# The m tiles' sums ahead of the tail in front, the last m tiles' work in block 0 laid out anew, and k's squares moved

## The chip, the cores and the metric

One core of a Trainium2 chip runs the whole program in one launch. The metric is the device time of that core in microseconds, the median of several executions. The kernel's times, its profile and its trace come from the same chip type. Line numbers (L288) are those of the kernel before.

## The reference

The reference computes a transformer-like block and all its gradients, for 2048 rows of width 512, 32 heads of 16 columns and an MLP of width 1792. In short:

```
xn = layernorm(x)
s  = attention(xn, wqkv) @ wo            # 32 heads, softmax over all 2048 keys
y  = layernorm(xn)
m  = gelu(y @ w1 + b1) @ w2 + b2
out = x + s * silu(m)
outputs: out, and the gradients of x, wqkv, wo, w1, b1, w2, b2 for a given grad_out
```

With `sg = sigmoid(m)` the gate is `m * sg`. The gradient that goes into attention's output is `dso = grad_out * m * sg`, and `dO = dso @ wo^T` is what attention's backward pass needs. The gradient towards m needs `s` and the factor `grad_out * sg * (1 + m * (1 - sg))`, so both `m * sg` and this factor are stored ("GB") for the last phase.

## The kernel before

The rows are cut into 16 tiles of 128, four tiles to a group. The program has three phases: `phase_pre` (layernorms, q, k, v, the MLP forward, the gate, dO), `attention_core` (attention forward and backward together) and `phase3` (the remaining products). Within `phase_pre` and within `attention_core` the order of the instructions on PE, ACT and DVE (in `phase_pre` on POOL too) is the order in which the code issues them; each engine works through its own list in that order and waits where an operand isn't there yet. The DMAs on SP's queue are placed by the framework.

**k's norms.** `kv_tile` makes k, v and q of one tile: three products on PE, three copies out of PSUM on ACT (L170), and after the fourth tile of a group three copies of k and v on POOL (L185 to L187) and a DMA. `k_norm(g, i)` squares k of one tile on POOL (L174) and sums the squares for each head on DVE (L175), through two buffers. The squares of groups 2 and 3 stand behind all of the `kv_tile` steps; behind them come a maximum over all tiles on DVE (L238) and one over the partitions on POOL (L239). The result is used in `row_shift`, which sets a bound for the exponent, much later.

**The MLP's hidden tiles.** `h_tile(g, fc)` is one of 14 tiles of the hidden layer for one group: four matmuls into one of seven PSUM banks (pool `psA`), the bias on DVE (9 of 14) or on ACT (5 of 14) into `h1p`, and for each pair of tiles one gelu on ACT and two DMAs to scratch memory (`H1T_s`, `HGT_s`). `h1p` has four buffers, each for a pair. Between the hidden tiles stand the norms of q (`q_norm`, POOL and DVE as for k) and, in groups 2 and 3, the dO products of tiles 0 to 7 (`do_proj`).

**The m tiles.** `m_tile(t)` issues, for one tile: 14 matmuls into a bank of `psA` (L284), the sum with b2 on DVE (`m_add`, L288), tanh and a scaled copy on ACT for the sigmoid (`m_sig`, L291 and L292), and then the tail on DVE: `m * sg` and `dso` (`m_dso`, L296 and L297) and three operations for the stored factor (`m_grad`, L307 to L309), followed by a DMA on POOL's queue (L310). After the last tile of a group `m_dso` also issues the DMA that transposes dso for the dO products (L301) and one that stores it (L303). Tiles 0 to 3 come after the hidden groups 0 and 1, tiles 4 to 7 after group 2, tiles 8 to 11 after group 3 and `row_shift`.

**Block 0.** Attention runs over 16 pairs of heads and four chunks of 512 queries: 64 blocks of 16 steps, one step for 128 keys. A step has the scores `s` (two matmuls into one of two PSUM slots of two banks, tag "st"), the products `d` (two banks of their own, `d0` and `d1`), the exp of s on ACT (`S`, L892), two products on DVE (`m0`, `m1`, L903) that read d and the exp, and the accumulating matmuls `a1` and `a2`. A second pass over each block, one block behind, uses `t` in the same "st" slots and an exp `T`; in 3 of its 16 steps the exp of t is not computed but the exp of s is transposed (`E`, L848, copied by DVE, `eE`, L853). One more PSUM bank, "z", serves E and the second pass. In block 0 there is no second pass yet, and `first_block` lays out a simpler order: step g issues s of g+2, E of g-1 where g is 4, 8 or 12, d of g+1, a1 of g, place V, a2 of g-1, place W. In the places V (index 0) and W (index 1) `left_over` puts the work on m tiles 12 to 15 and on dO of tiles 8 to 15, all through the z bank: the 14 matmuls of a tile in two halves (`first`, `second`), the sigmoid (`sig`) and the whole tail (`rest`) at V, dO one tile at a time (`do`), and the transpose of dso in four parts (`turn`) on PE, each copied by ACT (L392). dO's copy out of PSUM is on ACT too (L339).

Of the kernel before, what the change touches and what calls it, by code (L numbers as in the profile page):

```python
# [8 lines left out]
bf16 = mybir.dt.bfloat16  # L9
f32 = mybir.dt.float32  # L10
# [7 lines left out]
IC = D // 128  # L18
# [23 lines left out]
def phase_pre(ctx, tc, k, A_x, A_wqkv, A_wo, B_w1, B_b1, B_w2, B_b2, grad_out, opnds, psz, tailp):  # L42
# [157 lines left out]
    with tc.manual_schedule(engines={ET_.PE, ET_.Activation, ET_.DVE, ET_.Pool}):  # L200
        for g in range(2):
            load_x(g)
        nc.scalar.dma_start(out=wqkv_sb[:, :, D:3 * D], in_=wq3[:, :, D:3 * D])
        nc.scalar.dma_start(out=wqkv_sb[:, :, 0:D], in_=wq3[:, :, 0:D])
        nc.scalar.dma_start(out=w1_sb[:], in_=B_w1.rearrange("(c p) f -> p c f", p=128))
        for g in range(4):
            NS[g] = p1.tile([128, NPAIR, 4, 2, NATW], bf16, name="NS", bufs=4)
            nc.gpsimd.memset(NS[g][:, :, :, :, 0:1], 1.0)
        open1(0)
        open1(1)  # L210
        one_a(0, 0)
# [24 lines left out]
        for f, *a in steps:  # L236
            f(*a)
        nc.vector.reduce_max(out=kmaxrun[:], in_=kn2[:].rearrange("p t h -> p h t"), axis=AX.X)  # L238
# [63 lines left out]
        if i == 3:  # L302
            nc.sync.dma_start(out=k.DSO_s[g], in_=dso4[g])  # L303

    def m_grad(t, q, sg, gB):
        g, i = divmod(t, 4)
        nc.vector.scalar_tensor_tensor(out=q, in0=sg, scalar=1.0, in1=gB[:, 0, :], op0=ALU.subtract, op1=ALU.mult)  # L307
        nc.vector.tensor_tensor(out=q, in0=sg, in1=q, op=ALU.subtract)
        nc.vector.tensor_tensor(out=gB[:, 1, :], in0=q, in1=do4[g][:, i, :], op=ALU.mult)  # L309
        nc.gpsimd.dma_start(out=k.GB_s[g, :, i], in_=gB)  # L310

    def load_do(g):
        nc.sync.dma_start(out=do4[g], in_=rows4(go2, g))

    def m_tile(t):
        g, i = divmod(t, 4)
        if i == 0:
            do4[g] = p2.tile([128, 4, D], bf16, name="do4", bufs=1)[:]
            load_do(g)
            dso4[g] = p2.tile([128, 4, D], bf16, name="dso4", bufs=1)[:]  # L320
        m_mm(t, psA.tile([128, 512], f32, name="ps_m", tag="mm"), 0, FC)
        m = p2.tile([128, D], bf16, name="m")[:]
        m_add(t, m)
        th = p2.tile([128, D], f32, name="th")[:]
        sg = p2.tile([128, D], bf16, name="sg")[:]
        m_sig(m, th, sg)
        gB = p2.tile([128, 2, D], bf16, name="gB", bufs=3)[:]
        m_dso(t, m, sg, gB)
        m_grad(t, p2.tile([128, D], bf16, name="q1")[:], sg, gB)

    def do_proj(t, ps_pool=psA, tag="mm"):
# [4 lines left out]
        pd = ps_pool.tile([128, 512], f32, name="pd", tag=tag)  # L336
        for bc in range(IC):
            nc.tensor.matmul(pd[:], lhsT=dsoT[g][:, i, bc, :], rhs=woT[:, bc, :], start=(bc == 0), stop=(bc == IC - 1))
        nc.scalar.copy(out=nd[:, :, i, :], in_=pd[:].rearrange("p (a c) -> p a c", a=NPAIR))  # L339
        if i == 3:  # L340
            ts = slice(4 * g, 4 * g + 4)
            nd0 = nd[:, 0].rearrange("p t (j c) -> p t j c", j=2)
            nc.gpsimd.tensor_copy(out=QPad[:, ts, 2:4, 0:16], in_=nd0)
            if g >= 2:
                turn_q(g)
            nc.sync.dma_start(out=k.NATQd_s[g], in_=nd)
            nc.gpsimd.tensor_copy(out=OP0["NATQd"][:, ts], in_=nd0)

    def left_over(big, mid2, xt2):
# [12 lines left out]
        load_do(3)  # L362
        v = {}

        def z(nm):
            return psz.tile([128, 512], f32, name=nm, tag="z")

        def first(t):
            m_mm(t, z("ps_m15"), 0, 7)

        def second(t):
            m_mm(t, None, 7, FC)
            mq = mid2.tile([128, 2, 512], bf16, name="e")
            v[t] = dict(m=mq[:, 0, :], q=mq[:, 1, :])
            m_add(t, v[t]["m"])

        def sig(t):
            s = mid2.tile([128, 2, 512], bf16, name="e")
            v[t]["sg"] = s[:, 0, :]
            th = xt2.tile([128, 4, 128], f32, name="xt")  # L380
            m_sig(v[t]["m"], th[:].rearrange("p a b -> p (a b)"), v[t]["sg"])

        def rest(t):
            gB = gBs[:, t % 2]
            m_dso(t, v[t]["m"], v[t]["sg"], gB)
            m_grad(t, v[t]["q"], v[t]["sg"], gB)

        def turn(i):
            pt = psz.tile([128, IC, 128], bf16, name="dso_tp", tag="z")
            for b in range(IC):  # L390
                nc.tensor.transpose(pt[:, b, :], dso4[3][:, i, b * 128:(b + 1) * 128], k.ident_bf[:])
            nc.scalar.copy(out=dsoT[3][:, i], in_=pt[:])  # L392

        def do(t):
            do_proj(t, psz, "z")
        return {0: [[], [(first, 12)]], 1: [[], [(second, 12)]], 2: [[(sig, 12)], [(first, 13)]],
                3: [[(rest, 12)], [(second, 13)]], 4: [[(sig, 13)], [(first, 14)]], 5: [[(rest, 13)], [(second, 14)]],
                6: [[(sig, 14)], [(first, 15)]], 7: [[(rest, 14)], [(second, 15)]], 8: [[(sig, 15), (do, 8)], [(do, 9)]],
                9: [[(rest, 15), (do, 10)], [(do, 11)]], 10: [[(turn, 0)], [(turn, 1)]], 11: [[(do, 12)], [(turn, 2)]],
                12: [[(do, 13)], [(turn, 3)]], 13: [[(do, 14)], [(do, 15)]]}  # L400
# [22 lines left out]
    with tc.manual_schedule(engines={ET_.PE, ET_.Activation, ET_.DVE, ET_.Pool}):  # L423
# [5 lines left out]
        for fc in range(FC):  # L429
            h_tile(1, fc)  # L430
            if fc in (2, 4, 7, 9, 12):
                q_norm(qn.pop(0))
        for t in range(4):
            m_tile(t)
        for g in (2, 3):
            for fc in range(FC):
                h_tile(g, fc)
# [2 lines left out]
                elif fc in (1, 3, 5, 6, 8) or fc == 9 and g == 3:  # L440
                    q_norm(qn.pop(0))
            if g == 2:
                for t in range(4, 8):
                    m_tile(t)
# [3 lines left out]
        for t in range(8, 12):  # L448
            m_tile(t)
    c1.close()  # L450
    return left_over

# [322 lines left out]
def attention_core(ctx, tc, opnds, ps_z, tail, NAT_s, NATQ_s, Oall, dQall, dKVT_out, ident_f32, ident_bf, npairs=16, nqc=4, turned=(0, 1, 2)):  # L775
# [286 lines left out]
    p0, v0 = first_block()  # L1062
    pe = joined(p0, unrolled(PE_ORDER))
    dve = joined(v0, unrolled(DVE_ORDER))
    left = tail(gbp, ep, finp)
    act = []
    for g in range(NSTEP + 16):
        if g < NSTEP:
# [187 lines left out]
```

## Time and profile before

| | |
|---|---|
| median of 3 runs | 2359.58 us (2359.49 to 2362.84) |
| the profiled execution | 2358.28 us, of which its span is 2356.5 us |
| PE busy | 2232.8 us (95%) |
| DVE busy | 2025.0 us (86%) |
| ACT busy | 2044.4 us (87%) |
| POOL busy | 315.5 us (13%) |
| mean granted PE clock | 0.986 |

The span is what the trace covers; the 1.8 us beside it lie around it. PE's busy time counts matmuls that overlap in the array once. "Idle before" is the time that an engine stood before an instruction, and the arrow names what ended it. In the rows of the timeline the columns are start, duration, engine, line, operation, output and input tiles, shapes, number of instructions and, in brackets, the idle time.

### The profile page before, as it was taken

How to read it: one execution, taken by the hardware profiler on the slowest of the kernel's cores; microseconds unless marked ns; L12 is line 12 of the kernel's file. 1: busy time of each engine (PE TensorE's matmuls, PEld its weight loads, DVE VectorE, ACT ScalarE, POOL GpSimd, SP SyncE). 2: the span in 40 equal slices, each digit the busy share in tenths (PEclk: the TensorE clock that was granted, in tenths of full speed). 3: DMA queues.
4: the chain of work that ended last, by engine and by line, in shares of the span. 5: the costliest groups of instructions: out<-in, count | busy, mean ns of one | idle time of the engine just before them, and what ended most of it. 6: DMA issues, size and time to landing. Idle time of an engine off the chain costs nothing.

```text
span 2356.5 us, 50896 instructions
## 1 busy us (share of the span) xinstructions
PE 2232.8 (95%) x20082; PEld 796.0 (34%) x20128; DVE 2025.0 (86%) x3600; ACT 2044.4 (87%) x2336; POOL 315.5 (13%) x757
## 2 busy tenths in 40 slices
PE   7887999999999999999999999999999998889698
PEld 3332233333333333333333333333333333334343
DVE  6566899999999999999999999999999996775064
ACT  6564999999999999999999999999999998883143
POOL 4320111111111111111111111111111112100000
PEclk9998999999999999999999999999999999999899
DMA  9775999999999999999999989899999998796961
GB/s 294 226 265 130 173 164 181 171 168 182 164 180 166 184 163 178 168 176 169 177 176 166 183 161 190 158 182 167 178 167 177 156 155 220 192 214 123 187 161 63
DMA packets 1315362, 415.56 MB, mean 176 GB/s; under 512 B 1272241, under 2 KB 1291698, under 8 KB 1313970
## 3 DMA queue, kind: packets, MB, share of 16 engines
q1 hardware_dynamic: 1311362, 401.56, 89.9%
q0 software_dynamic: 2176, 7.34, 0.9%
q8 instruction: 157, 2.57, 0.4%
q10 hardware_dynamic: 1584, 3.41, 0.4%
q14 instruction: 83, 0.68, 0.1%
HBM read 46.52 MB, written 49.03 MB: 41 GB/s over the span
## 4 chain that ended last, share of the span: by engine, by line
PE 74%; DVE 9%; ACT 2%; issue 2%; SPq 2%; DMA 2%; DVEq 0%; ACTq 0%
PE d L886 12%; PE X L923 11%; PE s L864 11%; PE Z L1004 9%; PE X L936 7%; PE Z L996 5%; DVE gts L903 5%; PE t L876 5%; PE ET L848 4%; PE ps_dw L631 2%; PE XT L948 2%; PE X L926 1%; PE ps_dy L686 1%; PE ps_dwkv L736 1%; PE ps_dhg L646 1%
## 5 line engine op out<-in xcount | busy, mean ns | idle before, releaser
L903 DVE TENSOR_TENSOR gts<-d,et 128x512 bf16<-128x512 f32 x2048 | 1321.9, 684 | 79.8 <-PE d L886 25.9
L892 ACT ACTIVATE et<-s 128x1024 bf16<-128x1024 f32 x1024 | 1043.3, 1044 | 17.6 <-PE d L886 13.6
L897 ACT ACTIVATE e<-t 128x1024 bf16<-128x1024 f32 x832 | 866.4, 1042 | 22.0 <-PE t L876 3.5
L886 PE MATMUL d<-QDT,KVT 32*128 32x512 bf16 x2048 | 757.1, 384 | 20.6 <-DVE gts L903 19.5
L864 PE MATMUL s<-QDT,KVT 32*128 32x512 bf16 x2048 | 398.4, 385 | 11.3 <-DVE m L288 8.2
L1004 PE MATMUL Z<-gk,W 128*32 128x512 bf16 x2048 | 397.1, 384 | 0.0
L923 PE MATMUL X<-et,Lc 128*32 128x512 bf16 x2048 | 369.8, 389 | 0.0
L926 PE MATMUL X<-et,NAT 128*32 128x512 bf16 x2048 | 368.7, 388 | 0.0
L936 PE MATMUL X<-gts,NAT 128*17 128x512 bf16 x2048 | 330.9, 382 | 0.0
L996 PE MATMUL Z<-e,W 128*32 128x512 bf16 x1664 | 321.6, 383 | 3.6 <-DVE ob L1023 1.2
L876 PE MATMUL t<-KVT,QDT 32*128 32x512 bf16 x1664 | 323.1, 383 | 1.0 <-ACT e L897 1.0
L886 PEld LDWEIGHTS <-KVT 32*128 32x128 bf16 x2048 | 173.0, 90 | 236.5 <-issue 236.1
L864 PEld LDWEIGHTS <-KVT 32*128 32x128 bf16 x2048 | 106.0, 91 | 255.2 <-issue 230.8
L970 POOL TENSOR_TENSOR W<-NATQd,rL 128x128 bf16<-128x128 bf16 x64 | 25.8, 403 | 1122.0 <-DVE rL L969 1122.0
L1004 PEld LDWEIGHTS <-W 128*32 128x32 bf16 x2048 | 100.3, 94 | 171.8 <-issue 141.3
L876 PEld LDWEIGHTS <-QDT 32*128 32x128 bf16 x1664 | 92.1, 91 | 145.4 <-issue 140.6
L996 PEld LDWEIGHTS <-W 128*32 128x32 bf16 x2048 | 105.2, 94 | 106.8 <-issue 96.5
L923 PEld LDWEIGHTS <-Lc 128*32 128x32 bf16 x2048 | 83.6, 93 | 164.5 <-issue 164.3
L853 DVE COPY eE<-ET 128x1024 bf16<-128x1024 bf16 x192 | 130.2, 678 | 6.1 <-PE ET L848 6.1
L848 PE MATMUL ET<-ident_bf,et 128*128 128x128 bf16 x1536 | 119.0, 220 | 1.3 <-DVE e L288 0.9
L848 PEld LDWEIGHTS <-et 128*128 128x128 bf16 x1536 | 86.7, 98 | 44.7 <-issue 44.7
L936 PEld LDWEIGHTS <-NAT 128*17 128x17 bf16 x2048 | 79.6, 89 | 62.2 <-issue 45.6
(197 smaller groups left out, 2335.4 us busy)
## 6 DMA issues: line engine op xcount, KB each, us to landing
gk<-gts SPq DMA_TRANSPOSE x512, 4.5
H1T_s<-h1p SPq DMA_DIRECT2D x28, 256.0 KB, 3.1
h<-H1T_s SPq DMA_DIRECT2D x28, 256.0 KB, 3.3
HGT_s<-hgT SPq DMA_DIRECT2D x21, 256.0 KB, 2.5
NAT_s<-NS SPq DMA_DIRECT2D x4, 1056.0 KB, 5.7
dKVT_s<-ob SPq DMA_DIRECT2D x16, 256.0 KB, 3.7
gb<-GB_s SPq DMA_DIRECT2D x4, 1024.0 KB, 6.1
Rkv<-dKVT_s SPq DMA_DIRECT2D x2, 2048.0 KB, 13.2
```

The costliest lines, as they stand in the source:

```text
L848: nc.tensor.transpose(ET[:, hj, m * 128:(m + 1) * 128], st_et[g - 3 + m][:, hj, 384:512], ident_bf[:])
L864: nc.tensor.matmul(s[:, hj, :], lhsT=op["KVT"][r, kb * 128:(kb + 1) * 128], rhs=op["QDT"][r, qc * 512:(qc + 1) * 512], start=True, stop=Tr ...
L876: nc.tensor.matmul(t[:, hj, :], lhsT=op["QDT"][r, q0:q0 + 128], rhs=op["KVT"][r, kc * 512:(kc + 1) * 512], start=True, stop=True, tile_pos ...
L886: nc.tensor.matmul(d[:], lhsT=op["KVT"][r, kb * 128:(kb + 1) * 128], rhs=op["QDT"][r, qc * 512:(qc + 1) * 512], start=True, stop=True, til ...
L892: nc.scalar.activation(out=et[:], in_=st_s.pop(g)[:], func=ACT.Exp)
L897: nc.scalar.activation(out=e[:], in_=st_t.pop(g)[:], func=ACT.Exp)
L903: nc.vector.tensor_tensor(out=gts[:, g % 2, hj], in0=st_d.pop((g, hj))[:], in1=st_et[g][:, hj], op=ALU.mult)
L923: nc.tensor.matmul(X[64 + 32 * hj:96 + 32 * hj, :], lhsT=Lc[:, :], rhs=et[:, hj, :], start=(kb == 0), stop=False, skip_group_check=True, t ...
L926: nc.tensor.matmul(X[32 * hj:32 * hj + 32, :], lhsT=NATt[:, kb, hj, 1:33], rhs=et[:, hj, :], start=(kb == 0), stop=(kb == 15), tile_positi ...
L936: nc.tensor.matmul(X[64 + 32 * hj:64 + 32 * hj + 17, :], lhsT=NATt[:, kb, hj, 0:17], rhs=gts[:, kb % 2, hj, :], start=False, stop=(kb == 1 ...
L996: nc.tensor.matmul(Z[32 * hj:32 * hj + 32, :], lhsT=blk[j]["W1"][:, qb, hj, :], rhs=e[:, hj, :], start=(qb == 0), stop=False, tile_positio ...
L1004: nc.tensor.matmul(cur["Z"][32 * hj:32 * hj + 32, :], lhsT=blk[j]["W2"][:, qb, hj, :], rhs=grhs, start=False, stop=(qb == 3), tile_positio ...
```

## The change

- `k_norm` of groups 2 and 3 moves in between the last `kv_tile` steps; the maximum over all tiles moves behind the first hidden tile of group 1.
- `m_tile` becomes `m_group`: within a group of four tiles, a tile's sum and sigmoid are issued ahead of the tail of the tile in front.
- In block 0 the sigmoid is issued right after the sum (with `second`, at W of odd steps), and the tail is split: `rest1` (three DVE operations) at V of the next even step, `rest2` (two, and the DMA) at V of the odd step after it.
- dO is made two tiles at a time, and dso is transposed in one piece, both in the "st" slots of s; each is copied by one ACT instruction. They stand at W of steps 8 to 12.

The core of the diff:

```diff
-        steps += [(n2_c, 3, 0), (n2_c, 3, 1), (kv_tile, 3, 1), (n2_c, 3, 2), (n2_c, 3, 3), (kv_tile, 3, 2), (kv_tile, 3, 3)]
-        steps += [(k_norm, g, i) for g in (2, 3) for i in range(4)]
+        steps += [(n2_c, 3, 0), (n2_c, 3, 1), (kv_tile, 3, 1), (k_norm, 2, 0), (k_norm, 2, 1), (n2_c, 3, 2), (n2_c, 3, 3),
+                  (kv_tile, 3, 2), (k_norm, 2, 2), (k_norm, 2, 3), (k_norm, 3, 0), (k_norm, 3, 1), (kv_tile, 3, 3), (k_norm, 3, 2), (k_norm, 3, 3)]
         for f, *a in steps:
             f(*a)
-        nc.vector.reduce_max(out=kmaxrun[:], in_=kn2[:].rearrange("p t h -> p h t"), axis=AX.X)
-        nc.gpsimd.partition_all_reduce(kmax2[:], kmaxrun[:], channels=128, reduce_op=bass_isa.ReduceOp.max)
...
+    def m_grad1(t, q, sg, gB):
+        nc.vector.scalar_tensor_tensor(out=q, in0=sg, scalar=1.0, in1=gB[:, 0, :], op0=ALU.subtract, op1=ALU.mult)
+
+    def m_grad2(t, q, sg, gB):
         g, i = divmod(t, 4)
         nc.vector.tensor_tensor(out=q, in0=sg, in1=q, op=ALU.subtract)
         nc.vector.tensor_tensor(out=gB[:, 1, :], in0=q, in1=do4[g][:, i, :], op=ALU.mult)
         nc.gpsimd.dma_start(out=k.GB_s[g, :, i], in_=gB)
...
+    def m_group(g):
...
+        prev = None
+        for t in range(4 * g, 4 * g + 4):
+            m_mm(t, psA.tile([128, 512], f32, name="ps_m", tag="mm"), 0, FC)
+            m, sg, q = [p2.tile([128, D], bf16, name=nm)[:] for nm in ("m", "sg", "q1")]
+            gB = p2.tile([128, 2, D], bf16, name="gB", bufs=3)[:]
+            m_add(t, m)
+            m_sig(m, p2.tile([128, D], f32, name="th")[:], sg)
+            if prev:
+                m_dso(t - 1, prev[0], prev[1], prev[3])
+                m_grad(t - 1, prev[2], prev[1], prev[3])
+            prev = m, sg, q, gB
+        m_dso(t, prev[0], prev[1], prev[3])
+        m_grad(t, prev[2], prev[1], prev[3])
...
         def second(t):
             m_mm(t, None, 7, FC)
             mq = mid2.tile([128, 2, 512], bf16, name="e")
...
+            v[t] = mq[:, 1, :], s[:, 0, :], gBs[:, t % 2], mq[:, 0, :]
+            m_add(t, mq[:, 0, :])
             th = xt2.tile([128, 4, 128], f32, name="xt")
+            m_sig(mq[:, 0, :], th[:].rearrange("p a b -> p (a b)"), s[:, 0, :])
+
+        def rest1(t):
+            q, sg, gB, m = v[t]
+            m_dso(t, m, sg, gB)
+            m_grad1(t, q, sg, gB)
+
+        def rest2(t):
+            m_grad2(t, *v[t][0:3])
+
+        def turn(_):
+            pt = st2.tile([128, 4, IC, 128], bf16, name="dso_tp", tag="st")
+            for i in range(4):
+                for b in range(IC):
+                    nc.tensor.transpose(pt[:, i, b, :], dso4[3][:, i, b * 128:(b + 1) * 128], k.ident_bf[:])
+            nc.scalar.copy(out=dsoT[3], in_=pt[:])
 
         def do(t):
...
+            pd = st2.tile([128, 2, 512], f32, name="pd", tag="st")
+            for n in range(2):
+                for bc in range(IC):
+                    nc.tensor.matmul(pd[:, n, :], lhsT=dsoT[g][:, i + n, bc, :], rhs=woT[:, bc, :], start=(bc == 0), stop=(bc == IC - 1))
+            nc.scalar.copy(out=ND[g][:, :, i:i + 2, :].rearrange("p a n c -> p n a c"), in_=pd[:].rearrange("p n (a c) -> p n a c", a=NPAIR))
+            if i == 2:
+                do_done(g)
+        steps = {g: [[], []] for g in range(14)}
+        for n, t in enumerate(range(12, 16)):
+            steps[2 * n][1].append((first, t))
+            steps[2 * n + 1][1].append((second, t))
+            steps[2 * n + 2][0].append((rest1, t))
+            steps[2 * n + 3][0].append((rest2, t))
+        for g, f in ((8, (do, 8)), (9, (do, 10)), (10, (turn, 0)), (11, (do, 12)), (12, (do, 14))):
+            steps[g][1].append(f)
+        return steps
...
             h_tile(1, fc)
             if fc in (2, 4, 7, 9, 12):
                 q_norm(qn.pop(0))
-        for t in range(4):
-            m_tile(t)
+            if fc == 0:
+                nc.vector.reduce_max(out=kmaxrun[:], in_=kn2[:].rearrange("p t h -> p h t"), axis=AX.X)
+                nc.gpsimd.partition_all_reduce(kmax2[:], kmaxrun[:], channels=128, reduce_op=bass_isa.ReduceOp.max)
+        m_group(0)
```

`do_done(g)` holds what `do_proj` did after a group's last tile (the copies on POOL, for groups 2 and 3 the transposing DMA of `turn_q`, and the DMA that stores dO), unchanged.

More of the change, by code (lines that the diff above doesn't have):

```diff
@@ L303, in m_dso @@
             nc.sync.dma_start(out=k.DSO_s[g], in_=dso4[g])
-    def m_grad(t, q, sg, gB):
+    def m_grad1(t, q, sg, gB):
+        nc.vector.scalar_tensor_tensor(out=q, in0=sg, scalar=1.0, in1=gB[:, 0, :], op0=ALU.subtract, op1=ALU.mult)
+    def m_grad2(t, q, sg, gB):
         g, i = divmod(t, 4)
-        nc.vector.scalar_tensor_tensor(out=q, in0=sg, scalar=1.0, in1=gB[:, 0, :], op0=ALU.subtract, op1=ALU.mult)
         nc.vector.tensor_tensor(out=q, in0=sg, in1=q, op=ALU.subtract)
@@ L310, in m_grad, with do_proj @@
         nc.gpsimd.dma_start(out=k.GB_s[g, :, i], in_=gB)
+    def m_grad(*a):
+        m_grad1(*a)
+        m_grad2(*a)
     def load_do(g):
         nc.sync.dma_start(out=do4[g], in_=rows4(go2, g))
[L315 to L331, printed above, removed]
+    def m_group(g):
+        do4[g] = p2.tile([128, 4, D], bf16, name="do4", bufs=1)[:]
+        load_do(g)
+        dso4[g] = p2.tile([128, 4, D], bf16, name="dso4", bufs=1)[:]
+        prev = None
[11 more added lines that the diff above has]
+        m_grad(t, prev[2], prev[1], prev[3])
+    def do_proj(t):
         g, i = divmod(t, 4)
@@ L335, in do_proj @@
         nd = ND[g]
-        pd = ps_pool.tile([128, 512], f32, name="pd", tag=tag)
+        pd = psA.tile([128, 512], f32, name="pd", tag="mm")
         for bc in range(IC):
@@ L340, in do_proj, with do_done, left_over @@
         if i == 3:
[L341 to L349, printed above, removed]
+            do_done(g)
+    def do_done(g):
+        ts = slice(4 * g, 4 * g + 4)
+        nd0 = ND[g][:, 0].rearrange("p t (j c) -> p t j c", j=2)
+        nc.gpsimd.tensor_copy(out=QPad[:, ts, 2:4, 0:16], in_=nd0)
+        if g >= 2:
+            turn_q(g)
+        nc.sync.dma_start(out=k.NATQd_s[g], in_=ND[g])
+        nc.gpsimd.tensor_copy(out=OP0["NATQd"][:, ts], in_=nd0)
+    def left_over(big, mid2, xt2, st2):
         w = [big.tile([128, 2, 16, 128], bf16, name="gk")[:].rearrange("p a b c -> p (a b c)") for _ in range(3)]
@@ L383, in rest @@
[L383 to L392, printed above, removed]
-        def do(t):
[L395 to L400, printed above, removed]
+            m_sig(mq[:, 0, :], th[:].rearrange("p a b -> p (a b)"), s[:, 0, :])
@@ new lines, in do @@
+        def do(t):
+            g, i = divmod(t, 4)
+            pd = st2.tile([128, 2, 512], f32, name="pd", tag="st")
[4 more added lines that the diff above has]
+            if i == 2:
+                do_done(g)
@@ L442, in phase_pre @@
             if g == 2:
-                for t in range(4, 8):
-                    m_tile(t)
+                m_group(1)
         row_shift()
@@ L447, in phase_pre @@
         nc.scalar.activation(out=e_one[:], in_=k.eps_t[:], func=ACT.Exp)
-        for t in range(8, 12):
-            m_tile(t)
+        m_group(2)
     c1.close()
@@ L1064, in attention_core @@
     dve = joined(v0, unrolled(DVE_ORDER))
-    left = tail(gbp, ep, finp)
+    left = tail(gbp, ep, finp, ps_st)
     act = []
```

5 lines of the change are left out of this document (removed).

## The prediction

> **What bounds the kernel now.** I read the page first, then the busy times by stretches, then the timeline of the stretches that the diff touches.
>
> ```profile
> span 2356.5 us, 50896 instructions
> PEclk9998999999999999999999999999999999999899
> ...
> PE 74%; DVE 9%; ACT 2%; issue 2%; SPq 2%; DMA 2%; DVEq 0%; ACTq 0%
> ...
> L892 ACT ACTIVATE et<-s 128x1024 bf16<-128x1024 f32 x1024 | 1043.3, 1044 | 17.6 <-PE d L886 13.6
> ...
> H1T_s<-h1p SPq DMA_DIRECT2D x28, 256.0 KB, 3.1
> ...
> 75.00:80.00 5.00, 4.48 (x11) 1.62 (x11) 3.85 (x6) 4.34 (x5) 0.03 (x1) 0.50 0.86 303
> ...
> 270.20:297.40 27.20, 26.97 (x285) 8.91 (x286) 26.10 (x45) 26.90 (x30) 3.00 (x9) 1.00 0.98 169
> 188.49:212.70 24.21, 20.66 (x126) 6.73 (x128) 16.88 (x31) 11.00 (x13) 1.43 (x4) 0.91 0.54 126
> 212.70:239.74 27.04, 20.80 (x124) 7.61 (x126) 12.89 (x22) 13.29 (x19) 1.65 (x4) 0.87 0.59 128
> ...
> 75.00:95.00 20.00, 19.48 (x80) 8.39 (x80) 14.47 (x22) 18.66 (x22) 5.26 (x8) 0.87 0.93 343
> 107.00:127.00 20.00, 16.54 (x73) 7.10 (x73) 15.15 (x27) 11.40 (x15) 6.75 (x8) 1.00 0.64 209
> ```
>
> Of the page: the clock by slices, the engines' shares of the chain that ended last, an exp (1044 ns) and the writes of h1p with their landing time. Of the stretches, the columns are the stretch, its length, busy time of PE, PEld, DVE, ACT and POOL, granted PE clock, DMA share, GB/s. A steady attention block (270.20 to 297.40) has PE busy 26.97 of 27.20 us: nothing is to be had there, and the diff leaves its order alone. Everything it touches lies ahead of 243 us. There PE waits: 3.46 us of the 20 after the first group of m tiles, 3.55 and 6.24 us in the two halves of block 0, and it runs at half clock behind some of the waits. What is saved there moves the PE-bound rest forward whole.
>
> **The squares of k.**
>
> ```profile
> 55.76 2.04 POOL L174 TENSOR_TENSOR sq<-NS 128x512 f32<-128x512 bf16 x2 [0.69 <-DVE kn L175]
> 61.96 7.07 PE L266 MATMUL ps_h<-yT,w_sb 128*128 128x512 bf16 x32
> 63.91 0.31 POOL L185 COPY KPad<-NS 128x136 bf16<-128x136 bf16 x1 [6.12 <-ACT NS L170]
> 65.01 8.03 POOL L174 TENSOR_TENSOR sq<-NS 128x512 f32<-128x512 bf16 x8
> 66.08 0.69 DVE L175 TENSOR_REDUCE kn<-sq 128x32 f32<-128x512 f32 x1 [7.56 <-POOL sq L174]
> 66.78 5.63 SPq L427 DMA_TRANSPOSE KVT<-KPad  x1
> 73.79 1.02 DVE L238 TENSOR_REDUCE kmaxrun<-kn 128x32 f32<-128x512 f32 x1
> 74.73 3.37 DVE L269 TENSOR_SCALAR h1p<-ps_h,b1c 128x512 bf16<-128x512 f32 x5
> 75.52 19.77 PE L266 MATMUL ps_h<-yT,w_sb 128*128 128x512 bf16 x80 [6.49 <-DVE h1p L269]
> 75.53 0.33 SPq L274 DMA_DIRECT2D H1T_s<-h1p  x1
> ```
>
> Eight squares stand on POOL behind the last k and v tile, 1.0 us each; eight row sums and one maximum follow on DVE, and only then h1p, the reader that empties PE's banks. PE fills what it has by 69.03 and stands 6.49 us. POOL is free from 57.80 to 63.91 (55.76 + 2.04, then idle for 6.12 us until that tile's first copy). The change puts six squares into that hole (6 x 1.0 us: until 63.8), so the copies are not delayed; two stay behind them, 65.05 to 67.1, and their sums end at 67.8. The maximum goes behind the first h1p of the next group: 1.02 us of DVE beside PE, with DVE busy 14.47 of 20 us there. h1p then starts at 67.8 for 74.73, 6.9 us earlier, and at 68.5 a bank is free: PE never stands at 69.03.
>
> The half clock goes with the stall: in 75 to 80 us PE had 0.50 and 11 matmuls took some 0.43 us each, against 0.219 (12.25 us for 56 in the m tiles, quoted below): 11 x 0.21 = 2.3 us. Upper end: 6.5 + 2.3 = 8.8 us. [...]
>
> What is late next: h1p has four buffers, and the fifth waits for the first one's write, H1T_s. SP is held by the transpose of KVT until 72.41, so that write starts at about 72.5, 3.0 us earlier than 75.53, not 6.9. With 3.1 us to land, the fifth pair's first h1p runs from 75.6 to 76.3. PE's seven banks carry it over tiles 8 to 14, of 4 x 0.219 = 0.87 us, until 75.1: it waits 1.2 us, and its 20 tiles from 69.03 end at 87.6. The writes behind it come at 343 GB/s, 0.76 us each and two to a pair, 1.5 us for the 1.7 that PE needs for a pair. I add 0.8 for the loads that share the queues and put the first m tile at 88.4 instead of 94.9: 6.5 us. Lower end 3.0, if all writes keep their distance to the first one. ACT (18.66 busy of 20) starts seven us earlier on the same work and keeps pace.
>
> **The m groups.**
>
> ```profile
> 95.13 12.25 PE L284 MATMUL ps_m<-Oall,hgT 128*128 128x512 bf16 x54
> 98.35 0.69 DVE L288 TENSOR_TENSOR m<-ps_m,b2f 128x512 bf16<-128x512 f32 x1 [2.48 <-PE ps_m L284]
> 99.08 0.63 ACT L291 ACTIVATE th<-m 128x512 f32<-128x512 bf16 x1 [1.77 <-DVE m L288]
> 99.74 0.72 ACT L292 ACTIVATE sg<-th,half 128x512 bf16<-128x512 f32 x1
> 100.49 0.43 DVE L296 TENSOR_TENSOR gB<-m,sg 128x512 bf16<-128x512 bf16 x1 [1.45 <-ACT sg L292]
> 102.82 0.68 DVE L288 TENSOR_TENSOR m<-ps_m,b2f 128x512 bf16<-128x512 f32 x1
> 116.19 0.74 DVE L269 TENSOR_SCALAR h1p<-ps_h,b1c 128x512 bf16<-128x512 f32 x1
> ...
> 165.48 0.96 DVE L288 TENSOR_TENSOR m<-ps_m,b2f 128x512 bf16<-128x512 f32 x1
> 179.12 0.68 DVE L288 TENSOR_TENSOR m<-ps_m,b2f 128x512 bf16<-128x512 f32 x1
> 181.13 2.83 ACT L892 ACTIVATE et<-s 128x1024 bf16<-128x1024 f32 x3
> ```
>
> Each tile is one chain now: sum 0.69, ACT 1.4, tail 2.33 (100.49 to 102.82), 4.47 us in all (98.35 to 102.82), while PE makes a tile in 3.06 (12.25 / 4). With the next sum ahead of the tail, ACT runs beside the tail in front: DVE needs 0.69 + 2.33 = 3.02 a tile, and PE's 3.06 decides. From the first sum to the first h1p behind the group: 3 x 3.06 + 0.69 + 2 x 2.33 = 14.5 us for 17.84 (116.19 less 98.35): 3.3 us. PE's 3.46 idle us in the next 20 are this lateness, since its banks are emptied by that h1p and the q sums behind it. dO's transpose is issued 3.3 us earlier too, as its dso is. Groups 0 and 1: 2 x 3.3 = 6.6 us; ends 2 x 1.0 (the transpose or POOL's q squares come last instead) and 2 x 3.5 (all of PE's idle time).
>
> Group 2 ends in attention's start. PE's products are long there, as the first sum waits for the row shift: so from 165.48 sums 8 and 9 follow each other, tail 8 starts when ACT is through (167.9), and sum, tail, sum give sum 11 at 173.2 to 173.9 for 179.12. Its sigmoid ends at 175.3 and the first exp starts there, for 181.13: 5.8 us. Against it: when the first exp ended (182.1), DVE had 1.3 us of tail 11 left; now it has all 2.33 us. That takes 1.0: 4.8 us; ends 3.0 (both tails ahead of the first products) and 5.8.
>
> **Block 0.**
>
> ```profile
> 196.38 0.39 PE L864 MATMUL s<-QDT,KVT 32*128 32x512 bf16 x2
> ...
> 204.36 1.29 DVE L903 TENSOR_TENSOR gts<-d,et 128x512 bf16<-128x512 f32 x2 [3.23 <-PE d L886]
> ...
> 208.62 1.67 PE L284 MATMUL ps_m<-Oall,dQall 128*128 128x512 bf16 x6 [1.38 <-DVE e L288]
> ...
> 210.22 0.39 PE L864 MATMUL s<-QDT,KVT 32*128 32x512 bf16 x2
> 212.70 0.39 PE L864 MATMUL s<-QDT,KVT 32*128 32x512 bf16 x2
> 218.67 0.59 ACT L339 CAST gk<-pd 128x512 bf16<-128x512 f32 x1 [3.25 <-PE pd L338]
> ...
> 226.25 0.38 PE L391 MATMUL dso_tp<-ident_bf,gk 128*128 128x128 bf16 x4 [0.70 <-ACT gk L392]
> 230.06 0.61 PE L848 MATMUL ET<-ident_bf,et 128*128 128x128 bf16 x8 [0.35 <-ACT gk L392]
> 232.04 0.37 PE L886 MATMUL d<-QDT,KVT 32*128 32x512 bf16 x1 [1.38 <-DVE gts L903]
> ```
>
> Splitting the tail adds no instruction: DVE has 0.69 + 2.33 + 2 x 1.29 (two products each) = 5.6 us for two steps either way, against 5.0 of PE (2 x 2.48, from 210.22 to 212.70). What it removes is the one place where a sum stood behind a whole tail and held the z bank: 1.38 us. The stall at E (196.38, again in step 8) stays: E waits for the sum, d for E's copy. The sigmoid now stands ahead of the next exp on ACT and delays it by at most 0.69 + 1.4 = 2.1 us; that exp is read two steps later, so the two slots of s hide it; without them it would cost 2.1 a tile.
>
> In the second half, PE's work at full clock: 6 steps of 0.95 (2.48 less 7 x 0.219), 32 matmuls of dO 7.0, 16 transposes of dso at 0.095 1.5, two E's of 0.61; 15.4 us. The two E stalls cost some 2.0 each (the copy, then d behind the product, 1.38 and more): 4.0. dso's copy is now one of 2048 columns: 0.59 for 512 columns and an exp's 1.04 for 1024 give 0.59 + 3 x 0.45 = 1.9 us; dO's matmuls behind it wait some 0.9 of it. Lost to the clock at 0.87: 3.5. Sum 23.8 for 27.04. At the end ACT is behind by a dO copy (1.0 us), of which I count 0.7: gain 2.5. Gone are the short waits for ACT's copies in the z bank, 0.35 to 0.70 a time. Block 0: 1.4 + 2.5 = 3.9 us; ends -1 (s waits for each dO copy) and 9.8 (all PE idle time goes, 3.55 + 6.24).
>
> **The sum.** 6.5 + 6.6 + 4.8 + 3.9 = 21.8 us off the profiled execution's 2358.28 (span 2356.5): 2336.5. The shown median, 2359.58, is 1.3 above it, so I forecast 2337.8 as a median.
>
> **Rivals.** *The writes decide.* Squares give 3.0, the rest stays: 18.3, 2341.3. For it: the DMA share of 0.93 in 75 to 95; against it: PE has 17 us of work there anyway, and seven banks. *The clock stays up in block 0*, as the waits are shorter: 3.5 and the like from the first half (0.09 x 24.2 = 2.2) come on top, 27.5, 2332.1. Against it: both E stalls stay. *Slower: the steady block lengthens.* Five more tenants in the two slots of s and t shift their places; if a block's order no longer met its slots, each of the 63 blocks left would pay. From 21.8 / 63 = 0.35 us a block it decides; at 0.5 us, 31.5 - 21.8 = 9.7 slower, 2369. For it: PE has only 0.23 us to spare in a block. Against it: by the code a block has 16 s and 13 t, an odd number, so both places occur already. *It gives nothing*: the gains are taken back by the first long wait behind them, 2359; against it, the chain is PE for 74% of the span, and the block at 270 us has no wait for something that could be late from here.
>
> **Chances.** Forecast 0.65, with its own range 2331 to 2346; writes 0.14; clock 0.08; slower 0.08; nothing 0.05. The ends of the four terms add to 7 and 31.4 us; they hardly fall together, so the range is 2329 to 2350. A measurement tells 0.2%, 4.7 us, from no change: faster 0.87, same 0.05, slower 0.08.
>
> **What would show it.** Squares: no PE wait of 6 us ahead of the h tiles, and m's products from about 88.4 us. Groups: sums 3.06 us apart, and 14.5 us to the h1p behind. Start: the first exp 10 us after the group's first sum. Block 0: from step 1's end (the s at 188.49) to the s at 239.74 some 47 us for 51.25. A steady block of other than 27.2 us, or a PE wait of the same length right behind a removed one, would prove me wrong.

## The result, and the profile after

| | before | changed |
|---|---|---|
| median of 9 runs each | 2359.58 us (2356.79 to 2362.84) | 2352.88 us (2350.39 to 2355.10) |
| ratio, 95% interval | | 0.9969 (0.9958 to 0.9979) |
| the profiled execution, span | 2356.5 us | 2353.3 us |

The change makes the kernel 6.7 us faster: the direction of the forecast, and less than a third of its 21.8 us. The page of the changed kernel hardly differs in its totals (DVE is busy for 2024.0 us, 2025.0 before); the shares of the chain that ended last are these:

```profile
PE 76%; DVE 12%; issue 3%; DMA 3%; ACT 3%; SPq 2%; POOL 0%; ACTq 0%; DVEq 0%; POOLq 0%
```

DVE's share of the chain went from 9% to 12%, though DVE does no more work. The timeline of the changed kernel shows where (in its line numbers an h tile is L264, h1p L267, m's products L282, m's sum L286, a step's exp L915; columns as before):

```profile
54.86 8.02 POOL L174 TENSOR_TENSOR sq<-NS 128x512 f32<-128x512 bf16 x8 [0.69 <-DVE kn L175]
65.06 12.25 PE L264 MATMUL ps_h<-yT,w_sb 128*128 128x512 bf16 x56
65.67 2.04 POOL L174 TENSOR_TENSOR sq<-NS 128x512 f32<-128x512 bf16 x2
67.63 5.81 SPq L450 DMA_TRANSPOSE KVT<-KPad  x1
68.34 3.71 DVE L267 TENSOR_SCALAR h1p<-ps_h,b1c 128x512 bf16<-128x512 f32 x5
73.54 0.54 SPq L247 DMA_DIRECT2D b_bf<-in_B_b_dram  x1
74.12 0.42 SPq L317 DMA_DIRECT2D do<-in_grad_out_dram  x1
74.65 0.37 SPq L272 DMA_DIRECT2D H1T_s<-h1p  x1
80.34 0.75 DVE L267 TENSOR_SCALAR h1p<-ps_h,b1c 128x512 bf16<-128x512 f32 x1 [8.29 <-DMA H1T_s<-h1p]
81.15 11.34 PE L264 MATMUL ps_h<-yT,w_sb 128*128 128x512 bf16 x44 [3.84 <-DVE h1p L267]
81.71 0.62 POOL L835 COPY KPad<-NAT 128x512 bf16<-128x512 bf16 x1
85.66 1.03 DVE L457 TENSOR_REDUCE kmaxrun<-kn 128x32 f32<-128x512 f32 x1
88.19 0.45 POOL L458 PARTITION_ALL_REDUCE kmax<-kmaxrun  x1 [5.86 <-DVE h1p L267]
96.42 4.12 POOL L174 TENSOR_TENSOR sq<-NQ 128x512 f32<-128x512 bf16 x4 [7.78 <-issue]
97.48 0.69 DVE L175 TENSOR_REDUCE qn<-sq 128x32 f32<-128x512 f32 x1 [10.13 <-POOL sq L174]
98.88 4.19 PE L264 MATMUL ps_h<-yT,w_sb 128*128 128x512 bf16 x12 [6.39 <-DVE h1p L267]
102.90 12.25 PE L282 MATMUL ps_m<-Oall,hgT 128*128 128x512 bf16 x54
106.13 0.69 DVE L286 TENSOR_TENSOR m<-ps_m,b2f 128x512 bf16<-128x512 f32 x1 [0.98 <-PE ps_m L282]
109.15 0.69 DVE L286 TENSOR_TENSOR m<-ps_m,b2f 128x512 bf16<-128x512 f32 x1 [2.33 <-PE ps_m L282]
120.43 0.74 DVE L267 TENSOR_SCALAR h1p<-ps_h,b1c 128x512 bf16<-128x512 f32 x1
131.32 12.25 PE L282 MATMUL ps_m<-Oall,hgT 128*128 128x512 bf16 x55
159.74 12.25 PE L282 MATMUL ps_m<-Oall,hgT 128*128 128x512 bf16 x55
166.23 1.49 DVE L286 TENSOR_TENSOR m<-ps_m,b2f 128x512 bf16<-128x512 f32 x2
175.82 2.83 ACT L915 ACTIVATE et<-s 128x1024 bf16<-128x1024 f32 x3
```

Read it from the top. The squares moved as intended: h1p starts at 68.34 for 74.73. But then two waits of PE stand where one stood. SP issues the transpose of k, the load of b2 and a load of dO ahead of the first write of h1p, which goes out at 74.65 and lands 5.7 us later, at 80.34: PE waits 3.84 us. And POOL, between its last copy (81.71 + 0.62) and the squares of q at 96.42, does 0.45 us of work in 14 us: it waits 5.86 ahead of the all-reduce and 7.78 behind it, DVE waits 10.13 us for the square, PE 6.39 us for DVE. m's first product, forecast for 88.4, comes at 102.90, 7.8 us later than before's 95.13. The m groups and the start of attention went as forecast: the two groups shorten by 3.5 us each, and the first exp comes 9.6 us behind the group's first sum.

In the kernel before, the same all-reduce had the same gaps about it. In its timeline:

```profile
72.99 2.04 POOL L174 TENSOR_TENSOR sq<-NQ 128x512 f32<-128x512 bf16 x2
80.69 0.45 POOL L239 PARTITION_ALL_REDUCE kmax<-kmaxrun  x1 [5.65 <-issue]
81.02 0.69 POOL L250 CAST b2f<-b_bf 128x512 f32<-128x512 bf16 x1
90.23 3.03 POOL L174 TENSOR_TENSOR sq<-NQ 128x512 f32<-128x512 bf16 x3 [7.35 <-DVE h1p L269]
91.29 0.69 DVE L175 TENSOR_REDUCE qn<-sq 128x32 f32<-128x512 f32 x1 [1.01 <-POOL sq L174]
```

There two squares of q stood ahead of it, so DVE had something to sum until 90 and waited only 1.01 us for the third. By the code the all-reduce comes first there too, as the last instruction of one hand-ordered part of `phase_pre`, with q's squares in the next part; the trace shows that the written order does not hold across the two parts. The change puts the all-reduce inside the second part, where the order holds, and so ahead of every square of q. I had these rows in the trace and did not cost them.

Block 0, in the stretches of the changed kernel (stretch, length, busy PE, PEld, DVE, ACT, POOL, granted clock, DMA share, GB/s):

```profile
183.50:207.25 23.75, 21.72 (x126) 6.72 (x128) 16.93 (x31) 10.65 (x13) 1.10 (x3) 0.85 0.60 136
207.25:232.48 25.23, 19.45 (x125) 7.08 (x127) 12.36 (x22) 12.26 (x13) 1.90 (x6) 0.86 0.60 138
```

These two halves take 48.98 us for 51.25 before.

### The profile page after: what moved, and what is told of

It reads as the page before. It is cut to its first block, busy times and chain, and to the rows that moved or that the text cites. A ratio compares the mean times of both kernels' runs of the same rounds, so it can differ in the third digit from the quotient of the medians.

```text
span 2353.3 us, 50893 instructions
## 1 busy us (share of the span) xinstructions
PE 2235.4 (95%) x20082; PEld 796.2 (34%) x20128; DVE 2024.0 (86%) x3600; ACT 2043.5 (87%) x2329; POOL 314.8 (13%) x757
## 4 chain that ended last, share of the span: by engine, by line
PE 76%; DVE 12%; issue 3%; DMA 3%; ACT 3%; SPq 2%; POOL 0%; ACTq 0%; DVEq 0%; POOLq 0%
PE d L909 12%; PE X L946 11%; PE s L887 11%; PE Z L1027 9%; PE X L959 7%; DVE gts L926 5%; PE Z L1019 5%; PE ET L871 5%; PE t L899 4%; PE XT L971 2%; PE X L949 1%; PE ps_dy L709 1%; PE ps_dwkv L759 1%; PE ps_dw L654 1%; PE ps_m L282 1%
## 5 line engine op out<-in xcount | busy, mean ns | idle before, releaser
L915 ACT ACTIVATE et<-s 128x1024 bf16<-128x1024 f32 x1024 | 1044.8, 1046 | 11.4 <-PE d L909 11.1
```

The lines of the kernel that those rows point to most:

```text
L915: nc.scalar.activation(out=et[:], in_=st_s.pop(g)[:], func=ACT.Exp)
```

## The experiments

**Theory A**: the all-reduce in its new place stalls DVE and PE, some 8 to 9 us. **Theory B**: h1p's first write, held up on SP, costs another 5 to 6 us. **Rivals**: q's squares are late for another reason (R), or it is DVE's reduction, not POOL, that starts the stall. The ratios are to the kernel before on the same chip. Its median was 2360.28 us beside the maximum put back, moved alone, ahead of m's first group, and there with SP in written order; 2357.53 beside the maximum back with SP in written order and beside the three parts alone; 2362.73 beside the idle square; 2360.78 beside the other three. "SP in written order" means that the DMAs on SP's queue are no longer placed by the framework but issued where the code has them.

**The maximum put back** (all else as changed).

```diff
         for f, *a in steps:
             f(*a)
+        nc.vector.reduce_max(out=kmaxrun[:], ...)
+        nc.gpsimd.partition_all_reduce(kmax2[:], kmaxrun[:], ...)
...
-            if fc == 0:
-                nc.vector.reduce_max(...)
-                nc.gpsimd.partition_all_reduce(...)
```

> The changed kernel with one part undone: the maximum of k's norms (1.03 us on DVE, the all-reduce on POOL) stands again behind the last k/v tile, not behind the first h1p of group 1. Theory A (POOL needs some 6 us ahead of the all-reduce and 8 us behind it, and in its new place these stand ahead of q's squares, for which DVE and then PE wait): the DVE wait of 10.1 us ahead of q's row sums at 97.48 and the PE wait of 6.4 us at 98.88 go, m's first product comes at about 95 instead of 102.9, and the time is 2353 - 8 = 2345 us (2342 to 2348). Rival R (q's squares are late for another reason, as the norms' reads, and the all-reduce only shows beside them): the waits stay and the time is 2353 us. Theory B (h1p's first write, which lands 5.6 us behind its tile because SP stands at a transpose) says nothing here: its PE wait of 3.8 us at 81.15 stays.

Measured: 2343.80 us, ratio 0.9927 (0.9915 to 0.9940); 16.5 us off the kernel before instead of 6.7. Its timeline:

```profile
73.04 0.45 POOL L239 PARTITION_ALL_REDUCE kmax<-kmaxrun  x1 [6.37 <-issue]
80.83 13.84 PE L266 MATMUL ps_h<-yT,w_sb 128*128 128x512 bf16 x56 [6.32 <-DVE h1p L269]
85.51 2.03 POOL L174 TENSOR_TENSOR sq<-NQ 128x512 f32<-128x512 bf16 x2 [6.91 <-DMA H1T_s<-h1p]
94.51 12.25 PE L284 MATMUL ps_m<-Oall,hgT 128*128 128x512 bf16 x54
```

The gaps on POOL are still there (6.37 and 6.91), but earlier, where nobody waits for squares, and PE's second wait is gone. Theory A holds; R falls. PE's wait for the write stays, as B says.

**The maximum alone moved, in the kernel before.**

> The kernel before with one thing done: the maximum moved behind the first h1p of group 1. Theory A: DVE waits some 10 us for POOL's squares ahead of q's row sums, PE some 6 us ahead of an h tile of group 1, which the kernel before did not have, and the time is 2359.6 + 6 to 8 = 2366 to 2368 us. Rival R: POOL's all-reduce in this place is hidden, 2359 to 2360 us. What I forecast for this part alone was a gain of 1 us of DVE that hid beside PE: 2359 us.

Measured: 2369.63 us, ratio 1.0035 (1.0022 to 1.0047): 9.4 us slower by this edit alone. Its timeline has the same waits ahead of m's products (DVE's, at 98.03, is 10.21 us):

```profile
88.74 0.45 POOL L433 PARTITION_ALL_REDUCE kmax<-kmaxrun  x1 [6.02 <-DVE h1p L267]
96.97 4.12 POOL L174 TENSOR_TENSOR sq<-NQ 128x512 f32<-128x512 bf16 x4 [7.78 <-issue]
99.43 4.17 PE L264 MATMUL ps_h<-yT,w_sb 128*128 128x512 bf16 x12 [7.82 <-DVE h1p L267]
```

**POOL's all-reduce left out, DVE's maximum where the change has it** (`nc.vector.tensor_copy(out=kmax2[:], in_=kmaxrun[:])` in its place; the maximum over partitions is not formed).

> The changed kernel with the maximum where the change puts it, but POOL's all-reduce over the partitions left out: DVE copies the per-partition maxima instead, so the maximum over the 128 partitions is not formed. Theory A (it is POOL's time around the all-reduce, not DVE's reduction in that place): q's squares are there in time, PE's wait of 6.4 us goes, m's first product comes at 94 to 96 us, 9 us less than the changed kernel, a ratio of 0.993 to the kernel before. Rival (DVE's reduction of 1 us, in order ahead of the h1p that PE waits for, starts the stall): 0.997 as the changed kernel, the PE wait stays.

Measured: 2344.67 us, ratio 0.9930 (0.9917 to 0.9942), m's first product at 94.87; ahead of it PE has only the wait for the write (6.04 us at 80.95). POOL's squares have no gap ahead of them but DVE's pace. So it is POOL's time around the all-reduce that stalls PE, not DVE's reduction.

**The maximum right ahead of m's first group.**

> The changed kernel with the maximum right ahead of m's first group, where POOL has no squares left for 15 us. Theory A: as when it is put back, PE's wait of 6.4 us behind q's squares goes, m's first product at about 95, 2345 us (2342 to 2348). Rival R: the waits stay, 2353 us. A second way to lose: the all-reduce delays POOL's squares of group 2's q by its 14 us and a DVE wait for them shows up behind m's first group; then 2348 to 2353 us.

Measured: 2353.76 us, ratio 0.9969 (0.9957 to 0.9980): nothing gained. The forecast of 2345 us is missed; what came is the "second way to lose". m's first product came at 95.16, and the stall came back one group later, in its timeline:

```profile
97.62 0.45 POOL L457 PARTITION_ALL_REDUCE kmax<-kmaxrun  x1 [5.60 <-DVE kmaxrun L456]
113.06 0.54 POOL L310 DMA_DIRECT2D GB_s<-gB  x1 [1.78 <-DVE gB L309]
122.05 4.12 POOL L174 TENSOR_TENSOR sq<-NQ 128x512 f32<-128x512 bf16 x4 [8.44 <-issue]
123.11 0.69 DVE L175 TENSOR_REDUCE qn<-sq 128x32 f32<-128x512 f32 x1 [9.68 <-POOL sq L174]
124.50 1.87 PE L264 MATMUL ps_h<-yT,w_sb 128*128 128x512 bf16 x4 [8.29 <-DVE h1p L267]
```

The all-reduce ended at 98, 24 us ahead of the square, with four DMAs in between, and yet the square came 8.44 us after the last DMA. So the time behind an all-reduce is not spent when it ends but ahead of the next square (theory C). To try that:

**The same, with one idle square right behind the all-reduce.**

```diff
         nc.gpsimd.partition_all_reduce(kmax2[:], kmaxrun[:], ...)
+        nc.gpsimd.tensor_tensor(out=dummy[:]..., in0=NQ[:, :, 0, :, 1:17], in1=NQ[:, :, 0, :, 1:17], op=ALU.mult)
         m_group(0)
```

> The kernel with the maximum ahead of m's first group (2353.8 us on its chip, ratio 0.997), with one square more on POOL right behind the all-reduce, into a tile that nobody reads. Theory C: POOL pays its 7 to 9 us behind the all-reduce only ahead of the next square, so with a square at once it pays them at 98 to 107, while DVE works on m's tiles, and the squares of q in group 2 are there in time: DVE's wait of 9.7 us at 123.1 and PE's of 8.3 us at 124.5 go, ratio 0.993 to 0.994 (2344 to 2347 us). Against it: the DMAs of the stored factors, which POOL issues behind the new square, come 2 to 4 us later; their buffers are three. Rival: POOL's time behind the all-reduce is paid by whatever comes next and the group's DMAs had paid it already; then the new square changes nothing, ratio 0.997.

Measured: 2344.80 us, ratio 0.9927 (0.9913 to 0.9940). An instruction whose result nobody reads took 9 us out (2353.76 to 2344.80, medians of two chips; 0.0042 by the ratios). Its timeline:

```profile
97.68 0.45 POOL L457 PARTITION_ALL_REDUCE kmax<-kmaxrun  x1 [5.73 <-DVE kmaxrun L456]
105.09 1.18 POOL L459 TENSOR_TENSOR dummy<-NQ 128x512 f32<-128x512 bf16 x1 [6.95 <-issue]
106.22 0.74 POOL L310 DMA_DIRECT2D GB_s<-gB  x1
114.16 4.14 POOL L174 TENSOR_TENSOR sq<-NQ 128x512 f32<-128x512 bf16 x4
```

The 6.95 us are paid at once, beside m's tiles, and the squares at 114.16 follow the DMA without a gap.

**SP in written order, the maximum ahead of m's first group** (`ET_.SP` added to the engines of the hand-written order; the transpose of k then stands behind the ninth h tile, the loads of dO at the head of each m group).

> As the kernel with the maximum ahead of m's first group, and SP too in the order in which the block is written: the transpose of k and the loads of b2 and dO come behind the first writes of h1p, not ahead of them. Theory B (SP stands at the transpose from 67.6 to 73.5 us, and the write of h1p issued at 74.6 lands at 80.3): PE's wait of 3.8 us at 81.15 falls below 1 us and the half clock behind it shrinks; 2345 - 5 = 2340 us (2337 to 2343). Rival (PE's wait there is for the reads of H1T or for DVE, not for the write): 2345 us, the wait stays. Rival 2: the transpose or the dO load, now later, is waited for at the start of m's sums or of attention: 2345 us or more with such a wait in place of the old one.

Measured: 2359.47 us, ratio 0.9993 (0.9984 to 1.0002): another miss in the sum, by the all-reduce's stall in group 2 and by the expectation's rival 2, though theory B shows in its stage. The timeline:

```profile
72.52 0.46 SPq L272 DMA_DIRECT2D H1T_s<-h1p  x1
76.74 12.41 PE L264 MATMUL ps_h<-yT,w_sb 128*128 128x512 bf16 x56 [1.44 <-DVE h1p L267]
88.98 12.25 PE L282 MATMUL ps_m<-Oall,hgT 128*128 128x512 bf16 x54
122.17 1.86 PE L264 MATMUL ps_h<-yT,w_sb 128*128 128x512 bf16 x4 [7.79 <-DVE h1p L267]
178.82 0.43 DVE L295 TENSOR_TENSOR dso<-do,gB 128x512 bf16<-128x512 bf16 x1 [10.18 <-DMA do<-in_grad_out_dram]
```

The write goes out at 72.52, PE waits 1.44 us, and m's first product is at 88.98, 6.2 us earlier than with the same maximum and SP as changed. The all-reduce's stall in group 2 is there as before, and the loads of dO, now issued where they are written, come late: DVE waits 10.18 us at the start of attention.

**The maximum back, SP in written order, the loads of dO inside the h tiles ahead of their group** (in `row_shift` the store `NATQq_s` is also issued ahead of the two transposes of q).

> The kernel with the maximum put back (2343.8 us), and SP in the order in which the block is written, with the transpose of k behind the ninth h tile, and the loads of dO issued in the h tiles ahead of their group, so that they do not come late as in the run before. Theory B: the first write of h1p goes out at about 72.5, the PE wait of 6.3 us at 80.8 falls to some 1.4 us, m's first product at 88 to 89 us, and 2343.8 - 5.5 = 2338 us (2335 to 2341). Rival: what is gained ahead of m's first product comes back later as a wait for a load, as in the run before (2344 us or more, with a PE wait over 5 us somewhere between 89 and 180 us). Rival 2: the all-reduce now stands nearer to q's squares, and the DVE wait for them comes back: 2346 us or more.

Measured: 2335.57 us, ratio 0.9912 (0.9897 to 0.9926), 22 us off the kernel before by the medians, 21 by the ratio. The six executions lie at 2333.7 to 2335.8 and 2342.5 to 2343.6 us, and the profile is of the longest. Its timeline:

```profile
76.56 12.42 PE L266 MATMUL ps_h<-yT,w_sb 128*128 128x512 bf16 x56 [1.69 <-DVE h1p L269]
```

m's first product comes at 88.81 us behind this PE wait of 1.69; DVE still waits 3.00 us for the first load of dO, at 99.08.

**The same with that load seven h tiles earlier.**

> As the kernel before it (maximum back, SP in written order), with the first load of dO issued behind the fifth h tile of group 1 instead of the twelfth: there DVE waited 3.0 us for it at 99.1 and m(0) to m(4) took 32.2 us instead of 28.4. If that wait is what the load costs, m(0) to m(4) takes 28.4 us again and the ratio to the kernel before falls from 0.991 to 0.990 or 0.989 (22 us less becomes 24 to 26 us less). Rival: the load, earlier, holds up the writes of h1p behind it, a PE wait of over 1 us comes ahead of m's first product, and the time stays.

Measured: ratio 0.9906 (0.9893 to 0.9919), 2339.62 us beside 2360.78. From first h tile to m's first product PE has no wait left (65.49 to 89.73, 112 matmuls in one row of its timeline), and m(0) to m(4) takes 29.6 us instead of 32.2; DVE now waits 2.70 us for a write of h1p in there. The times don't tell the two apart.

**The parts alone, in the kernel before.** k's squares:

> The kernel before with k's squares moved and nothing else; the maximum stays behind the last k/v tile. My prediction gave this part 6.5 us: 2353 us. With theory B the squares' gain stands ahead of h1p's first write and is eaten there: PE waits 6 us ahead of an h tile as before, for the write instead of for DVE, m's first product comes 0 to 1.5 us earlier than 95.1, and the time is 2358 to 2360 us. The rival in the prediction in which the writes decide: 3 us, 2356.5 us.

m's sums:

> The kernel before with m's sums ahead of the tail of the tile in front, and nothing else. By the trace of the changed kernel: 3.5 us for each of two groups and 5.7 us at the start of attention, 12.7 us in all, 2347 to 2348 us (my prediction's terms: 6.6 + 4.8 = 11.4 us, 2348 to 2349 us). Rival (the gain at the start of attention needs the squares' or block 0's part): 7 us, 2353 us.

block 0:

> The kernel before with block 0's tail in two parts, dO by pairs and the turn in one, and nothing else. My prediction's term: 3.9 us, 2355.7 us. By the traces block 0 is worth 2.3 us where the granted clock falls in the two steps that build E (48.98 us for 14 steps, the changed kernel), and 4.8 us where it does not (46.43 us, the kernel with the maximum put back): 2355 to 2358 us. Rival: the part does nothing by itself, since the steady steps behind it set the pace: 2360 us.

| part alone | ratio, 95% interval | off the kernel before | forecast |
|---|---|---|---|
| k's squares | 0.9983 (0.9974 to 0.9991) | 4.0 us | 6.5 us |
| m's sums | 0.9955 (0.9937 to 0.9973) | 10.6 us | 6.6 + 4.8 us |
| block 0 | 0.9984 (0.9976 to 0.9993) | 3.8 us | 3.9 us |
| the maximum (above) | 1.0035 (1.0022 to 1.0047) | 8.3 us more | 0 |

(The third column is one less the ratio, times the kernel before's median on that chip.) The four add to 10.1 us less, for 7.3 together by the ratio (0.0031 x 2359.58); without the maximum to 18.4, for 17.2 in the kernel with the maximum put back (0.0073 x 2360.28). The squares' 4.0 us are not seen in their trace: PE waits 6.26 us for the write ahead of an h tile, as theory B has it, and m's first product comes at 96.01. So the time that theory B gave, 2358 to 2360 us, is missed (median 2353.66; the profiled execution took 2356.73), and where those microseconds come from I leave open.

**SP in written order with early loads, in the kernel before.**

> The kernel before with SP in written order and the loads of dO ahead, and nothing of the change. Theory B says that the write only decides once the squares no longer do: before, h1p on DVE starts at 74.7 behind k's squares, when SP is free, so m's first product stays at 94 to 96 us and the ratio is 0.999 to 1.001. Rival (the writes decide in the kernel before too): 0.997 to 0.998, m's first product at 90 to 92 us.

Measured: 2367.11 us, ratio 1.0022 (1.0014 to 1.0031), m's first product at 95.09. That the write decides nothing there is right; that the edit is free is a miss. Its timeline:

```profile
87.16 0.67 POOL L817 COPY KPad<-NAT 128x544 bf16<-128x544 bf16 x1 [5.75 <-DMA KVT<-KPad]
96.21 3.03 POOL L174 TENSOR_TENSOR sq<-NQ 128x512 f32<-128x512 bf16 x3 [7.83 <-issue]
97.27 0.69 DVE L175 TENSOR_REDUCE qn<-sq 128x32 f32<-128x512 f32 x1 [5.39 <-POOL sq L174]
```

The later transpose holds a copy on POOL, behind which the 7.83 us ahead of the next square begin, and now DVE waits 5.39 us for the square.

## Why the prediction was wrong

**The step that failed** is one sentence: "The maximum goes behind the first h1p of the next group: 1.02 us of DVE beside PE, with DVE busy 14.47 of 20 us there." It costed the half of the moved work that runs on DVE, and left out the instruction that moves with it on POOL, the all-reduce, and what then stands behind it: all of q's squares, where two had stood ahead. In its place the runs showed 14 us of POOL around the all-reduce (5.86 + 0.45 + 7.78), for which DVE waits 10.13 us and PE 6.39. Made alone, the move of the maximum costs 9.4 us by the medians and 8.3 by the ratio; undone in the changed kernel, it gives 9 us (2352.88 to 2343.80, ratio 0.9969 to 0.9927). The gap ahead of the all-reduce is 5.59 us (SP in written order in the kernel before) to 6.37 us (the maximum put back) in nine kernels. The second gap, ahead of the next square, is the longer of the two: 6.89 us (the maximum back, SP in written order) to 8.79 us (SP in written order, the maximum ahead of m's first group). What either of them consists of, no run here shows.

**The write of h1p** was the right wait and mis-sized. "That write starts at about 72.5" and has "3.1 us to land", it says; it started at 74.65, behind two loads that I had not looked for on SP's queue, and took 5.7 us. (With SP in written order it goes out at 72.52 us, and the h1p that waits for it starts 3.4 us later, at 75.93. Why it took 5.7 us behind the transpose and the loads is not shown.) PE waits 3.84 to 6.32 us for it in the kernels with the squares moved and SP's order as it was, and with the maximum put back the gain ahead of m's first product is 0.6 us (95.13 to 94.51), not 6.5. With SP in written order it is 6.3 us (88.81, behind a PE wait of 1.69), nearly the forecast's 88.4 behind 1.2. The rival in which the writes decide had this mechanism, but left the squares 3.0 us where 0.6 came.

**The half clock** goes with the stall, as forecast. In the first 5.00 us behind the wait of 6.49 us (75.52 to 80.52, the kernel before) the granted clock is 0.52; behind the changed kernel's wait of 3.84 us it is 0.66 (81.15 to 86.15), then 1.00 (86.15 to 92.49), and the 44 matmuls take 0.258 us each (11.34 / 44). Behind the wait of 1.69 us (the maximum back, SP in written order) 56 take 0.222 us each (12.42 / 56), and where PE has no wait left, the 112 matmuls take 0.216 us each (24.24 us from 65.49 to 89.73). The forecast's 2.3 us for it are part of its upper end of 8.8 us alone: the 6.5 us of the sum are counted from m's first products, 94.9 to 88.4.

**The m groups** were right: m(0) to m(4) 28.42 us for 31.95, m(4) to m(8) 28.42 for 31.98: 3.5 and 3.6 us for 3.3. The sums are 3.02 apart, and 14.30 us lie from the first to the h1p behind (106.13 to 120.43; forecast 14.5).

**The start** was right: from the group's first sum to the first exp 9.59 us for 15.65 (forecast 10); from m(8) to the s at step 1's end 23.76 us for 29.43, 5.7 us for 4.8.

**Block 0** was right over the profiles and not in this one. The 14 steps take 48.98 us here, but 46.43 in the kernel with the maximum put back and 46.44 with block 0 alone; over nine profiles with the new layout 45.27 to 49.09, median 46.45, and over five with the old one 51.22 to 53.84. Forecast 47 for 51.25. The waits are those that it named: none ahead of m's products any more, 1.38 us for d behind E's copy, 1.09 behind dso's copy (forecast 0.9). Among the nine, DVE's and ACT's work is the same within 0.3 us; what differs is the clock (next section but one): 0.86 in the three that took 48.82 us or more, 0.90 to 0.92 in the other six. The rival in which the clock stays up falls: in the two halves it was 0.85 and 0.86, for 0.91 and 0.87 before.

**The rival in which the steady blocks lengthen** falls. From the s that ends these 14 steps to the end of the span lie 2115.8 to 2120.8 us in the nine profiles with the new layout, mean 2118.9, and 2113.0 to 2123.8 in the five with the old one, mean 2118.3. This scatter of some 10 us in a part that no edit touches is also why one profile says less than the medians: before and after differ by 7.3 us at block 0's end and by 3.2 at the span's.

**The sum**, with measured terms: squares and maximum together 7.8 us later in the trace (3.1 of it already at the first h tile, 61.96 to 65.06; that tile starts between 61.96 and 63.96 in the profiles with the squares where they were, between 62.19 and 65.49 with them moved, so most of the 3.1 is scatter), groups 7.1, start 5.7, block 0 2.3 earlier: 7.3 us, for 6.7 by the medians. With the maximum put back and SP in written order, the gain is 21 to 22 us, what the forecast had, but of a kernel for which it had not been made.

## What to carry to other kernels

When an edit moves an operation, list what it issues on each engine and, on each of those engines, what then stands behind it; an engine that is busy 13% of the time, as POOL is here, still sets the pace where its next result is awaited (10.13 us of DVE, 6.39 of PE). Look in the trace of before for idle time around the moved instruction itself: the 5.65 and 7.35 us were there to be read, hidden by two squares that stood ahead, and in another order than the code's. A long gap that comes with a kind of instruction can be moved to where nobody waits, even by an extra instruction: here 6.95 us to 105.09, for 8.44 us ahead of 122.05, and the ratio went from 0.9969 to 0.9927.

## What the runs showed of the hardware

**An all-reduce on POOL, with a square behind it, costs POOL 13 to 15 us, of which the profile counts 0.45 as busy** (nine kernels; 5.73 + 0.45 + 6.89 = 13.07 with the maximum back and SP in written order, 5.80 + 0.45 + 8.79 = 15.04 with SP in written order and the maximum ahead of m's first group). Ahead of it POOL stands 5.59 to 6.37 us from the end of its earlier work, and this runs beside DVE (with the maximum ahead of m's first group 97.62 less 5.60 is 92.0, ahead of the maximum that ends at 96.9). Behind it a cast and copies follow at once (81.02 and 81.59 in the kernel before), and a DMA 0.3 us behind its operand (104.70, after DVE's product that ends at 104.40, with the maximum ahead of m's first group). But the next TENSOR_TENSOR, a square, comes 6.89 to 8.79 us after whatever stands in front of it, even when the all-reduce ended 24 us earlier (8.44 us at 122.05, with the maximum ahead of m's first group). One whose result nobody reads takes this on itself (6.95 us at 105.09). Squares that stand behind a DMA with no all-reduce in between have no such gap (114.16 with the idle square).

**The same step of block 0 ran at different clocks in kernels whose code for it is the same.** From d of the second step that builds E, through the first dO products, to the next s, in the stretches of the changed kernel and of the one with the maximum put back:

```profile
210.09:215.00 4.91, 4.68 (x16) 1.19 (x16) 3.13 (x6) 0.28 (x1) 0.00 (x0) 0.65 0.43 83
```

```profile
200.80:204.07 3.27, 3.04 (x16) 0.90 (x15) 3.13 (x6) 0.29 (x1) 0.00 (x0) 1.00 0.08 16
```

The same 16 matmuls keep PE busy for 4.68 of 4.91 us at a granted clock of 0.65, and for 3.04 of 3.27 at 1.00. The waits ahead of them are the same (1.38 us for d behind E's copy). So the order of the work alone doesn't settle where the clock falls; it is worth 1.6 us here (4.68 less 3.04), and by my estimate up to 3.8 us over block 0 (45.27 to 49.09 over the nine profiles). What does settle it, the runs don't show.
